# Query loads moved from ScalarE's queue to SyncE's and spread over the strip, the norm's arithmetic moved from GpSimd to VectorE, and the sums of W_in in another order

## The chip, the cores and the metric

The kernel runs on one core of a Trainium2 chip. A core has TensorE (PE, matrix products, with its weight loads shown apart as PEld), VectorE (DVE), ScalarE (ACT), GpSimd (POOL) and SyncE (SP, which here only issues DMAs). Each has its own instruction stream, and they meet at semaphores. An engine works through its stream in order, so an instruction that waits holds up all that stand behind it on the same engine. SBUF is the working memory, PSUM the memory into which PE writes its products; "HBM" is the memory outside.

The metric is device time in microseconds, the median of several runs. The profile is of one further run.

## The reference

Two blocks are chained. The first is linear attention without a softmax; each head's output is divided by its root mean square:

```python
kv = np.einsum('bhsd,bhse->bhde', k, v)
out = np.einsum('bhsd,bhde->bhse', q, kv)
rms = np.sqrt(np.mean(out * out, axis=-1, keepdims=True) + 1e-06)
return (out / rms * g_norm).astype(np.float32)
```

with 8 batches, 8 heads, 576 positions and 64 features. The heads of a position are put side by side, which gives x with 4608 rows and 512 columns. The second block is a feed-forward layer with 2048 hidden features:

```python
h = x @ w_in
r = np.maximum(h, 0.0)
g = r * r
return (g @ w_out).astype(np.float32)
```

All is in 32-bit floats; the two weight matrices come as 64-bit floats and are converted in the kernel.

## The kernel before

**Tiles and strips.** The 4608 rows of x are 36 tiles of 128 rows, and four tiles make a strip, so there are nine strips, numbered 0 to 8. For each strip the kernel computes h = x W_in (the first products, "up"), the squared relu, and g W_out (the second products, "down"). Both products use Strassen's scheme: seven products of half-size blocks in place of eight, at the price of sums of blocks. From strip 1 on the down products, and from strip 2 on the up products too, use it twice over (`up_small`, `small_products`). Sums of weights are made once: `sums_in` (line 269) and `deep_sums_in` (line 1040) make those of W_in. The first are made by VectorE at the end of strip 0, after ScalarE has scaled W_in by the norm's weight. The second are made by GpSimd in strip 1 and are written to HBM (`w_in_deep`). Weight blocks (`w_blk`) stream back in through four buffers, by SyncE.

**Attention inside the strips.** While PE works through strip s, the attention for strip s+1 is done in between. It is cut into small slices, a list `slices` of functions with arguments; after each step of a strip, `attend` (line 680) runs as many slices as are due. In strips from 2 on a step of the up products is called a slot (`up_slot`), and all slices are due within the first 37 of 55 slots. So all attention work falls into the up products. The slices for batch b are:

- `key_value`: k'v for two heads at a time, on PE; ScalarE copies it to SBUF (`kv_all`, lines 382 and 383). It then issues the load of the k and v that come two pairs later.
- `transposed_query(b, p)` (line 346): from batch 2 on VectorE transposes the queries of head pair p (line 350) from tile `q` to `qT`. Tile `q` has two buffers, so the load for a pair can't start until the pair two before it is transposed. The last quarter of a row tile has its queries in `q_rest`.
- `query(pair)`: the products of queries with k'v for two tiles (line 411, `x_ps`, one PSUM buffer), and their squares on ScalarE (line 420, `sq`).
- `mean_roots`: VectorE reduces the squares (line 428), GpSimd makes mean and epsilon (line 429), ScalarE takes the root (line 434, `rms`).
- `roots`: VectorE takes the reciprocal (line 440) and GpSimd does one Newton step in four small instructions (lines 441 to 444)[...].
- `normalized`: VectorE multiplies `x_ps` by the result (line 491), which frees `x_ps`.
- `squares_x`, `send_x`, `fetch_x`: a transposition in blocks on VectorE (line 558), a write to HBM and a read back (lines 567 and 573), which together put x into `xT` with features on the partitions.

**Query loads.** One pair's queries are four DMAs (`load`, line 121) and the `q_rest` of one batch eight (line 167). `load_queries` and `load_q_rest` are slices as well: `transposes` puts one of them into `later_q` for every transpose, and `turn` lets one out at a time among the other slices. They are issued on ScalarE's queue (`nc.scalar`). All DMAs of the program, whatever queue they are in, share eight semaphores in turn; a DMA is not issued until the one that had its semaphore before has landed.

**PSUM in the up products.** There are five banks for products (`fpsum`), one bank with tag "at", in which k'v products are made, and the two of `x_ps`. Each product's bank is emptied by ScalarE (line 1151, `snap`) or by VectorE (line 1146), and PE waits for that before it writes the bank again. GpSimd adds earlier results to some of the copies (line 1146) and makes the sums of x (`x_l`, `x_t`, line 262).

Lines 1206 and following are the loop over a strip's steps, with the calls of `attend`, `sums_in`, `sums_x` and `deep_sums_in`.

Of the kernel before, what the change touches and what calls it, by code (L numbers as in the profile page):

```python
# [10 lines left out]
FP32 = mybir.dt.float32  # L11
# [4 lines left out]
ALU = mybir.AluOpType  # L16
# [4 lines left out]
def kernel(  # L21
# [34 lines left out]
    nc = tc.nc  # L56
    P = 128
# [4 lines left out]
    NP = H // 2  # L62
# [37 lines left out]

    main = {}

    def load(b, p, q_eng, names="kvq"):
        hs = slice(2 * p, 2 * p + 2)
        inputs = (("q", q, q_eng), ("k", k, nc.sync), ("v", v, nc.sync))
        if b == 0 and p >= 2:

            h_place = g_pool.tile([P, 4, C * P], FP32, name="first_qkv", tag="gt")
        if b == 1 and p == 2:
            h_place = spare_pool.tile([P, 3, C * P], FP32, name="more_qkv")  # L110
        placed = (b, p) in ((0, 2), (0, 3), (1, 2))
        for i, (n, src, eng) in enumerate(inputs if b == 0 else inputs[1:] + inputs[:1]):
            if n not in names:
                continue
            whole = src[b, hs, 0 : C * P].rearrange("h (sp c) d -> sp h c d", c=C)
            if n == "q" and b >= Q_ON_PE:

                t = qkv_pool.tile([P, 4 * C, SQ], FP32, name=n, tag=n)
                for a in range(4):
                    h, f = divmod(a * SQ, D)  # L120
                    eng.dma_start(
                        out=t[ts(a, SQ)],
                        in_=src[b, 2 * p + h, 0 : C * P, f : f + SQ].rearrange("(i k) f -> i k f", k=4 * C),
                    )
            elif n != "q":
                if placed:
                    t = h_place[:, i].rearrange("p (h c d) -> p h c d", h=2, c=C)
                else:
                    t = qkv_pool.tile([P, 2, C, D], FP32, name=n, tag=n)
                eng.dma_start(out=t, in_=whole)  # L130
            else:

                if placed:
                    t = h_place[:, i].rearrange("p (c h d) -> p c h d", h=2, c=C)
                else:
                    t = qkv_pool.tile([P, C, 2, D], FP32, name=n, tag=n)
# [15 lines left out]
        for t, src in ((k_rest[half], k), (v_rest[half, h], v)):  # L152
            eng.dma_start(out=t, in_=src[b, :, C * P : S].rearrange("h s d -> s h d"))

    def load_q_rest(b, eng, half=None):
        h = b % 2
        if h == 0 and not half:
            q_rest[b // 2] = rest_pool.tile([P, H, D], FP32, name="q_rest", tag="q_rest")
        src = q[b, :, C * P : S]
        if b < Q_ON_PE:  # L160
            eng.dma_start(out=q_rest[b // 2][REST * h : REST * (h + 1)], in_=src.rearrange("h s d -> s h d"))
            return
        t = squares(q_rest[b // 2])
        for a in range(*((0, 4) if half is None else (2 * half, 2 * half + 2))):
            hq, f = divmod(a * SQ, D)
            for kq in range(2):
                eng.dma_start(
                    out=t[ts(a, SQ), 2 * h + kq], in_=src[hq::2, ts(kq, SQ), f : f + SQ].rearrange("p i f -> i p f")
                )
# [9 lines left out]
            load(*u, q_eng, names)  # L179
            owed.extend([u] if "q" not in names else [])  # L180

    def load_queries():
        if owed:
            load(*owed.popleft(), nc.scalar, "q")


    KH, FH, DH = NP // 2, d_ff // 2, d_model // 2
# [156 lines left out]
            nc.tensor.matmul(ps, lhsT=ident, rhs=ident[:, : ps.shape[1]], start=True, stop=True)  # L344

    def transposed_query(b, p):
        t = main.pop(("q", b, p))
        if b >= Q_ON_PE:
            qT[b, p] = qt_pool.tile([P, C, P], FP32, name="qT", tag="qT")
            nc.vector.transpose(out=flat(qT[b, p]), in_=flat(t))  # L350
            if b % 2 and p == NP - 1:
                nc.vector.transpose(
                    out=open_rest(b).rearrange("p q (k t) -> p q k t", k=4),
                    in_=squares(q_rest[b // 2]).rearrange("p k q f -> p q k f"),
                )
            return
        ps = apsum.tile([P, C, P], FP32, name="t_ps", tag="at")
        if (b, p) == (0, 0):
            keep_busy(ps[:, 0], 8)
        for c in range(C):  # L360
            nc.tensor.transpose(ps[:, c, :], flat(t[:, c]), ident)
        qT[b, p] = qt_pool.tile([P, C, P], FP32, name="qT", tag="qT")
        nc.scalar.copy(qT[b, p], ps)
# [56 lines left out]
            nc.scalar.activation(sqs[-1], ps, AF.Square)  # L420
        return sqs

    def mean_of(sqs, eng=nc.vector):
        ms = small.tile([P, 2, H], FP32, name="ms", tag="ms")[:, : len(sqs)]
        for i, sq in enumerate(sqs):
            if len(sq.shape) == 3:
                sq = sq.rearrange("p r e -> p (r e)")
            nc.vector.reduce_sum(out=ms[:, i], in_=by_head(sq), axis=AX.X)
        eng.tensor_scalar(out=ms, in0=ms, scalar1=1.0 / D, scalar2=EPS, op0=ALU.mult, op1=ALU.add)
        return ms  # L430

    def root_of(ms):
        r = small.tile([P, 2, H], FP32, name="rms", tag="rms")[:, : ms.shape[1]]
        nc.scalar.activation(r, ms, AF.Sqrt)
        return r

    def newton(ms, r):

        t = small.tile([P, 2, H], FP32, name="newton", tag="newton")[:, : ms.shape[1]]
        nc.vector.reciprocal(r, r)  # L440
        nc.gpsimd.tensor_tensor(out=t, in0=ms, in1=r, op=ALU.mult)
        nc.gpsimd.tensor_tensor(out=t, in0=t, in1=r, op=ALU.mult)
        nc.gpsimd.tensor_scalar(out=t, in0=t, scalar1=-0.5, scalar2=1.5, op0=ALU.mult, op1=ALU.add)
        nc.gpsimd.tensor_tensor(out=r, in0=t, in1=r, op=ALU.mult)
        return r

    def inverse_root(ms, r):
# [2 lines left out]

        nc.vector.scalar_tensor_tensor(out=t, in0=ms, scalar=-0.5, in1=r, op0=ALU.mult, op1=ALU.mult)
        nc.vector.tensor_tensor(out=t, in0=t, in1=r, op=ALU.mult)
        nc.vector.scalar_tensor_tensor(out=r, in0=t, scalar=1.5, in1=r, op0=ALU.add, op1=ALU.mult)
        return r

    queried = []

# [11 lines left out]

    def roots_normalized(ns):  # L470
        parts, ms = queried.pop()
        queried.append((parts, inverse_root(ms, root_of(ms))))
        normalized(ns)

    def mean_roots(ns):
        parts, sqs = queried.pop()
        ms = mean_of(sqs, nc.gpsimd)
        queried.append((parts, (ms, root_of(ms))))

    def roots(ns):  # L480
        parts, means = queried.pop()
        queried.append((parts, newton(*means)))

    def normalized(ns):
        parts, r = queried.pop()
        for i, n in enumerate(ns):
            x_n[n] = xn_pool.tile([P, d_model], FP32, name="x_n", tag="x_n")
            o = x_n[n].rearrange("p (q r d) -> p r q d", r=2, d=D)
# [134 lines left out]
    for pair in query_pairs(1):  # L623
        slices += [(query_means, (pair,)), (roots_normalized, (pair,))]
        for n in pair:
# [4 lines left out]
            slices.append((features, (n,)))  # L630
            if n % NT == NT - 1:
                ready[n // NT] = len(slices)
    load_q = (load_queries, ())
    later_q = deque()

    def transposes(b, ps_of):
        for p in ps_of:
            slices.append((transposed_query, (b, p)))
            later_q.append(load_q)
            if p == NP - 1 and b + 1 < B:  # L640
                later_q.extend((load_q_rest, (b + 1, nc.scalar, half)) for half in range(2))

    def turn(n=1):
        for _ in range(min(n, len(later_q))):
            slices.append(later_q.popleft())

    for b in range(2, B):
        if b > 3:
            fetch(2)
            transposes(b, (2, 3))  # L650
        else:
            for p in range(NP):
                turn()
                slices.append((key_value, (b, p)))
                transposes(b, (p,))
                fetch(1)
                if b == 2 and p == 0:
                    slices += late
        for i, pair in enumerate(query_pairs(b)):
            slices.append((query, (pair, *((b + 1, 2 * i, 2 * i + 1) if i < 2 < b < B - 1 else ()))))  # L660
            if i == (2 if b % 2 else 1) and 2 < b < B - 1:
                transposes(b + 1, (0, 1))
            else:
                turn()
            slices.append((mean_roots, (pair,)))
            fetch(1)
            turn()
            slices.append((roots, (pair,)))
            fetch(1)
            turn()  # L670
            slices.append((normalized, (pair,)))
            for n in pair:
                turn()
                slices.append((squares_x, (n,)))
            slices += [(send_x, (n,)) for n in pair]
            fetches.extend(pair)
    fetch(2)
# [506 lines left out]
    for s in range(N_STRIP):  # L1184
# [21 lines left out]
        for i, (w, fn, a) in enumerate(steps):  # L1206
# [26 lines left out]
                convert((3, 4, 5, 7)[i])  # L1233
            done += w
            if s:
                if s >= DEEP_UP:
                    attend(begun + (goal - begun) * min(i + 1, 37) // 37)
                else:
# [1 line left out]
                if s == DEEP and i == n_up - 3:  # L1240
                    leaf_sums(s, 4)
                if s == 1 and i in range(6, 27, 3):
                    deep_sums_in(i // 3 - 2)
                if s == 1 and i == n_up - 2:
                    stream(2)
                continue
# [4 lines left out]
            if i == n_up + 9:  # L1251
                load_rest(2, nc.sync)
                load_q_rest(2, nc.sync)
            if i - n_up in (7, 9, 10, 12):
                sums_in((i - n_up - 6) // 2)
            if i == n_up + 11:
                sums_x(1)
            n = i + 1 - (n_up - 6)
            pairs, m = divmod(max(n - 2 * NP, 0), 3)
# [34 lines left out]
```

## Time and profile before

| | us |
|---|---|
| median of 3 runs | 982.31 (980.74 to 984.03) |
| profiled run, span | 973.3 |
| PE busy | 903.6 |
| DVE busy | 722.6 |
| ACT busy | 319.4 |
| POOL busy | 322.2 |

How to read the profile: the span is divided among busy and idle time of each engine. An instruction that only waits, or that issues a DMA, does not count as busy; in the answers such work is marked with a q after the engine, as in ACTq. A group's or an instruction's arrow "<-" names what it waited for. "PEclk" is the clock that TensorE was granted, in tenths of full speed. "L1151" is line 1151 of the kernel. The page cuts the span into 40 slices of about 24.3 us. A strip from 2 on takes some 90 to 110 us, and of this the down products are about 39.

### The profile page before, as it was taken

How to read it: one execution, taken by the hardware profiler on the slowest of the kernel's cores; microseconds unless marked ns; L12 is line 12 of the kernel's file. 1: busy time of each engine (PE TensorE's matmuls, PEld its weight loads, DVE VectorE, ACT ScalarE, POOL GpSimd, SP SyncE). 2: the span in 40 equal slices, each digit the busy share in tenths (PEclk: the TensorE clock that was granted, in tenths of full speed). 3: DMA queues.
4: the chain of work that ended last, by engine and by line, in shares of the span. 5: the costliest groups of instructions: out<-in, count | busy, mean ns of one | idle time of the engine just before them, and what ended most of it. 6: DMA issues, size and time to landing. Idle time of an engine off the chain costs nothing.

```text
span 973.3 us, 20802 instructions
## 1 busy us (share of the span) xinstructions
PE 903.6 (93%) x8246; PEld 841.0 (86%) x8246; DVE 722.6 (74%) x1198; ACT 319.4 (33%) x646; POOL 322.2 (33%) x390
## 2 busy tenths in 40 slices
PE   6999996899978899889997999899899999999998
PEld 5434885789968898889997999799899999999998
DVE  3898978459836795558864896489568976895796
ACT  3796341230023701154023601270028014501720
POOL 0000003080417604352336404550456048315710
PEclk8999998999989999999998999899999999999999
DMA  9599997959897487776887687849755866685475
GB/s 279 210 290 297 308 345 225 218 203 331 305 247 195 166 311 251 189 210 232 300 211 213 218 321 229 215 157 331 222 176 178 315 223 218 231 315 195 141 278 188
DMA packets 173807, 235.72 MB, mean 242 GB/s; under 512 B 85008, under 2 KB 138768, under 8 KB 165264
## 3 DMA queue, kind: packets, MB, share of 16 engines
q1 hardware_dynamic: 121168, 227.84, 70.3%
q10 hardware_dynamic: 52544, 6.56, 4.7%
q8 instruction: 65, 1.06, 0.4%
q14 instruction: 30, 0.25, 0.1%
HBM read 197.66 MB, written 36.70 MB: 241 GB/s over the span
## 4 chain that ended last, share of the span: by engine, by line
PE 60%; DMA 13%; DVE 12%; POOL 4%; issue 4%; ACT 3%; SPq 2%; ACTq 2%; DVEq 0%; POOLq 0%
PE ps_B L946 19%; PE ps_A L946 15%; PE ps_A L1134 11%; PE ps_B L1134 5%; DMA q<-in_q_dram 4%; PE ps_C L1134 3%; DMA w_blk<-w_in_deep 2%; PE ps_A L725 2%; POOL gt L1146 2%; DVE w_t L262 2%; PE kv_ps L379 1%; DVE o_sb L961 1%; DVE w_c L242 1%; DMA v_rest<-in_v_dram 1%; DMA w_out<-w_in 1%
## 5 line engine op out<-in xcount | busy, mean ns | idle before, releaser
L1134 PE MATMUL ps_A<-x_l,w_in 128*128 128x128 f32 x784 | 109.3, 284 | 18.8 <-ACT snap L1151 18.5
L946 PE MATMUL ps_B<-w_blk,g_s 128*128 128x128 f32 x1024 | 126.0, 275 | 0.0
L946 PEld LDWEIGHTS ps_B<-w_blk,g_s 128*128 128x128 f32 x1024 | 120.0, 192 | 0.1
L1134 PEld LDWEIGHTS ps_A<-x_l,w_in 128*128 128x128 f32 x784 | 98.6, 197 | 21.7 <-ACT snap L1151 14.3
L946 PE MATMUL ps_B<-w_blk,gt 128*128 128x128 f32 x768 | 97.4, 275 | 0.0
L946 PE MATMUL ps_A<-w_blk,g_s 128*128 128x128 f32 x768 | 93.6, 275 | 0.0
L946 PEld LDWEIGHTS ps_B<-w_blk,gt 128*128 128x128 f32 x768 | 91.5, 192 | 0.1
L262 POOL TENSOR_TENSOR x_l<-xT 128x256 f32<-128x256 f32 x21 | 15.7, 748 | 223.4 <-PE ps_A L946 223.3
L946 PEld LDWEIGHTS ps_A<-w_blk,g_s 128*128 128x128 f32 x768 | 89.6, 192 | 0.0
L1151 ACT COPY snap<-ps_A 128x512 f32<-128x512 f32 x63 | 36.5, 582 | 153.9 <-PE ps_A L1134 89.4
L1146 POOL TENSOR_TENSOR snap<-snap,gt 128x512 f32<-128x512 f32 x35 | 45.9, 1312 | 118.5 <-ACT snap L1151 79.8
L961 DVE TENSOR_TENSOR o_sb<-o_sb,ps_B 128x256 f32<-128x256 f32 (+1 forms) x128 | 49.5, 387 | 35.4 <-ACT o_sb L962 27.9
L1084 ACT ACTIVATE gt<-gt 128x512 f32<-128x512 f32 x112 | 69.6, 622 | 15.3 <-DVE gt L1146 11.0
L946 PE MATMUL ps_A<-w_blk,gt 128*128 128x128 f32 x576 | 72.2, 275 | 0.0
L1085 ACT ACTIVATE gt<-gt 128x512 f32<-128x512 f32 x112 | 70.6, 631 | 3.6
L946 PEld LDWEIGHTS ps_A<-w_blk,gt 128*128 128x128 f32 x576 | 68.2, 192 | 0.0
L1044 POOL TENSOR_TENSOR w_i<-w_in 128x512 f32<-128x512 f32 x7 | 9.8, 1394 | 156.2 <-PE kv_ps L379 153.8
L262 DVE TENSOR_TENSOR gt<-gt 128x2048 f32<-128x2048 f32 (+1 forms) x29 | 59.7, 2063 | 0.0
L1146 POOL TENSOR_TENSOR gt<-gt,snap 128x512 f32<-128x512 f32 x42 | 52.4, 1276 | 16.0 <-DVE snap L1146 15.8
L1134 PE MATMUL ps_A<-x_l,w_blk 128*128 128x128 f32 x392 | 53.8, 281 | 3.8 <-POOL x_l L262 3.8
L962 ACT COPY o_sb<-ps_A 128x128 f32<-128x128 f32 x24 | 6.4, 266 | 146.0 <-PE ps_A L946 146.0
L1134 PEld LDWEIGHTS ps_A<-x_l,w_blk 128*128 128x128 f32 x392 | 49.2, 197 | 4.8 <-POOL x_l L262 4.3
(177 smaller groups left out, 1856.3 us busy)
## 6 DMA issues: line engine op xcount, KB each, us to landing
w_blk<-w_deep SPq DMA_DIRECT2D x56, 1024.0 KB, 6.4
w_blk<-w_out SPq DMA_DIRECT2D x56, 768.0 KB, 5.7
w_blk<-w_in_deep SPq DMA_DIRECT2D x49, 768.0 KB, 5.2
raw<-in_moe_w_in_dram SPq DMA_DIRECT2D x16, 512.0 KB, 6.5
raw<-in_moe_w_out_dram SPq DMA_DIRECT2D x16, 512.0 KB, 5.9
k<-in_k_dram SPq DMA_DIRECT2D x29, 256.0 KB, 4.8
v<-in_v_dram SPq DMA_DIRECT2D x29, 256.0 KB, 5.0
x_d<-x_q SPq DMA_DIRECT2D x27, 256.0 KB, 3.3
```

What stands on the lines that cost most here:

```text
L242: yield nc.vector.scalar_tensor_tensor(out=ci, in0=high, scalar=-(2**30), in1=ci, op0=ALU.bitwise_and, op1=ALU.bitwise_or)
L262: eng.tensor_tensor(out=out, in0=a, in1=b, op=ALU.subtract)
L379: nc.tensor.matmul(ps[ts(h, D), i], lhsT=a, rhs=w, start=c == 0, stop=c == C)
L725: nc.tensor.matmul(bank[BANK[p]][:, i, :], lhsT=lhsT(k), rhs=rhs(k), start=p in (1, 5, 2) and i == 0 and k == 0, stop=k == n - 1, skip_gro ...
L946: nc.tensor.matmul(chain[c][x][:, i, :], lhsT=a[:, f, :], rhs=w[:, f, :], start=x not in opened[c] and f == 0, stop=f == FQ // 2 - 1, skip ...
L961: add = lambda out, a, b: nc.vector.tensor_tensor(out=out, in0=a, in1=b, op=ALU.add)
L1044: nc.gpsimd.tensor_tensor(out=s1, in0=w_half(b, 0, 1), in1=w_half(b, 1, 1), op=ALU.add)
L1084: nc.scalar.activation(o, o, AF.Relu)
L1085: nc.scalar.activation(o, o, AF.Square)
L1134: nc.tensor.matmul(ps[:, i, :], lhsT=w, rhs=rhs, start=j in (1, 2, 5) and i == 0, stop=True, skip_group_check=True)
L1146: add = lambda eng, out, a, b: eng.tensor_tensor(out=out, in0=a, in1=b, op=ALU.add)
L1151: nc.scalar.copy(t, ps)
```

## The change

There are three parts.

1. Query loads go to SyncE's queue. They are no longer slices. Each transpose of a pair puts the load of the next pair that is owed into a queue `drips`, in two halves of two DMAs each; the last transpose of a batch puts in the next batch's `q_rest`, in four parts of two DMAs. At every second step of a strip, up and down products alike, `drip` lets one part out. A transpose lets out what it needs itself if that is still waiting. The aim is to keep DMA issues off ScalarE and to spread them.
2. The mean, epsilon and the Newton step are done on VectorE. The slice `roots` is gone, and its work is done in `normalized`. ScalarE writes the root into PSUM, in the bank with tag "at". The aim is a shorter chain between engines.
3. Sums of W_in. `sums_in` of the four groups comes after down steps 7, 8, 9 and 11 of strip 0, where it was 7, 9, 10 and 12, and the sums of x come after step 12, where it was 11. `deep_sums_in` takes the seven blocks in the order 1, 6, 5, 4, 0, 2, 3.

```diff
-    def load_queries():
+    drips = deque()
+
+    def drip(n=1):
+        for _ in range(min(n, len(drips))):
+            f, a = drips.popleft()
+            f(*a)
+
+    def drip_queries():
         if owed:
-            load(*owed.popleft(), nc.scalar, "q")
+            u = owed.popleft()
+            drips.extend((load, (*u, nc.sync, "q", (2 * h, 2 * h + 1))) for h in range(2))
...
     def transposed_query(b, p):
+        while any(a[:2] == (b, p) for _, a in drips):
+            drip()
         t = main.pop(("q", b, p))
...
             if b % 2 and p == NP - 1:
+                while any(f is load_q_rest and a[0] == b for f, a in drips):
+                    drip()
...
+            drip_queries()
+            if p == NP - 1 and b + 1 < B:
+                drips.extend((load_q_rest, (b + 1, nc.sync, a)) for a in range(4))
             return
...
-    def mean_of(sqs, eng=nc.vector):
+    def mean_of(sqs):
...
-        eng.tensor_scalar(out=ms, in0=ms, scalar1=1.0 / D, scalar2=EPS, op0=ALU.mult, op1=ALU.add)
+        nc.vector.tensor_scalar(out=ms, in0=ms, scalar1=1.0 / D, scalar2=EPS, op0=ALU.mult, op1=ALU.add)
...
-    def newton(ms, r):
-
-        t = small.tile([P, 2, H], FP32, name="newton", tag="newton")[:, : ms.shape[1]]
-        nc.vector.reciprocal(r, r)
-        nc.gpsimd.tensor_tensor(out=t, in0=ms, in1=r, op=ALU.mult)
-        nc.gpsimd.tensor_tensor(out=t, in0=t, in1=r, op=ALU.mult)
-        nc.gpsimd.tensor_scalar(out=t, in0=t, scalar1=-0.5, scalar2=1.5, op0=ALU.mult, op1=ALU.add)
-        nc.gpsimd.tensor_tensor(out=r, in0=t, in1=r, op=ALU.mult)
-        return r
...
     def mean_roots(ns):
         parts, sqs = queried.pop()
-        ms = mean_of(sqs, nc.gpsimd)
-        queried.append((parts, (ms, root_of(ms))))
-
-    def roots(ns):
+        ms = mean_of(sqs)
+        r = apsum.tile([P, 2, H], FP32, name="root", tag="at")[:, : len(ns)]
+        queried.append((parts, (ms, root_of(ms, r))))
+
+    def normalized(ns):
         parts, means = queried.pop()
-        queried.append((parts, newton(*means)))
-
-    def normalized(ns):
-        parts, r = queried.pop()
+        r = inverse_root(*means)
...
             if s:
+                if i % 2 == (i >= n_up):
+                    drip()
...
                 if s == 1 and i in range(6, 27, 3):
-                    deep_sums_in(i // 3 - 2)
+                    deep_sums_in((1, 6, 5, 4, 0, 2, 3)[i // 3 - 2])
...
-            if i - n_up in (7, 9, 10, 12):
-                sums_in((i - n_up - 6) // 2)
-            if i == n_up + 11:
+            if i - n_up in (7, 8, 9, 11):
+                sums_in((7, 8, 9, 11).index(i - n_up))
+            if i == n_up + 12:
                 sums_x(1)
```

More of the change, by code (lines that the diff above doesn't have):

```diff
@@ L101, with load @@
     main = {}
-    def load(b, p, q_eng, names="kvq"):
+    def load(b, p, q_eng, names="kvq", parts=range(4)):
         hs = slice(2 * p, 2 * p + 2)
@@ L116, in load @@
             if n == "q" and b >= Q_ON_PE:
-                t = qkv_pool.tile([P, 4 * C, SQ], FP32, name=n, tag=n)
-                for a in range(4):
+                t = qkv_pool.tile([P, 4 * C, SQ], FP32, name=n, tag=n) if 0 in parts else main[n, b, p]
+                for a in parts:
                     h, f = divmod(a * SQ, D)
@@ L153, in load_rest, with load_q_rest @@
             eng.dma_start(out=t, in_=src[b, :, C * P : S].rearrange("h s d -> s h d"))
-    def load_q_rest(b, eng, half=None):
+    def load_q_rest(b, eng, one=None):
         h = b % 2
-        if h == 0 and not half:
+        if h == 0 and not one:
             q_rest[b // 2] = rest_pool.tile([P, H, D], FP32, name="q_rest", tag="q_rest")
@@ L163, in load_q_rest @@
         t = squares(q_rest[b // 2])
-        for a in range(*((0, 4) if half is None else (2 * half, 2 * half + 2))):
+        for a in range(4) if one is None else (one,):
             hq, f = divmod(a * SQ, D)
@@ L428, in mean_of, with root_of @@
             nc.vector.reduce_sum(out=ms[:, i], in_=by_head(sq), axis=AX.X)
-        eng.tensor_scalar(out=ms, in0=ms, scalar1=1.0 / D, scalar2=EPS, op0=ALU.mult, op1=ALU.add)
+        nc.vector.tensor_scalar(out=ms, in0=ms, scalar1=1.0 / D, scalar2=EPS, op0=ALU.mult, op1=ALU.add)
         return ms
-    def root_of(ms):
-        r = small.tile([P, 2, H], FP32, name="rms", tag="rms")[:, : ms.shape[1]]
+    def root_of(ms, ps=None):
+        r = ps if ps is not None else small.tile([P, 2, H], FP32, name="rms", tag="rms")[:, : ms.shape[1]]
         nc.scalar.activation(r, ms, AF.Sqrt)
-        return r
-    def newton(ms, r):
-        t = small.tile([P, 2, H], FP32, name="newton", tag="newton")[:, : ms.shape[1]]
-        nc.vector.reciprocal(r, r)
-        nc.gpsimd.tensor_tensor(out=t, in0=ms, in1=r, op=ALU.mult)
-        nc.gpsimd.tensor_tensor(out=t, in0=t, in1=r, op=ALU.mult)
-        nc.gpsimd.tensor_scalar(out=t, in0=t, scalar1=-0.5, scalar2=1.5, op0=ALU.mult, op1=ALU.add)
-        nc.gpsimd.tensor_tensor(out=r, in0=t, in1=r, op=ALU.mult)
         return r
@@ L452, in inverse_root @@
         nc.vector.tensor_tensor(out=t, in0=t, in1=r, op=ALU.mult)
-        nc.vector.scalar_tensor_tensor(out=r, in0=t, scalar=1.5, in1=r, op0=ALU.add, op1=ALU.mult)
-        return r
+        nc.vector.scalar_tensor_tensor(out=t, in0=t, scalar=1.5, in1=r, op0=ALU.add, op1=ALU.mult)
+        return t
     queried = []
@@ L471, in roots_normalized @@
         parts, ms = queried.pop()
-        queried.append((parts, inverse_root(ms, root_of(ms))))
+        queried.append((parts, (ms, root_of(ms))))
         normalized(ns)
@@ L632 @@
                 ready[n // NT] = len(slices)
[L633 to L645, printed above, removed]
     for b in range(2, B):
@@ L649 @@
             fetch(2)
-            transposes(b, (2, 3))
+            slices += [(transposed_query, (b, p)) for p in (2, 3)]
         else:
             for p in range(NP):
-                turn()
-                slices.append((key_value, (b, p)))
-                transposes(b, (p,))
+                slices += [(key_value, (b, p)), (transposed_query, (b, p))]
                 fetch(1)
@@ L661 @@
             if i == (2 if b % 2 else 1) and 2 < b < B - 1:
-                transposes(b + 1, (0, 1))
-            else:
-                turn()
+                slices += [(transposed_query, (b + 1, p)) for p in (0, 1)]
             slices.append((mean_roots, (pair,)))
             fetch(1)
-            turn()
-            slices.append((roots, (pair,)))
+            slices.append((normalized, (pair,)))
             fetch(1)
[L670 to L674, printed above, removed]
+            slices += [(squares_x, (n,)) for n in pair]
             slices += [(send_x, (n,)) for n in pair]
```

## The prediction

> **What bounds the kernel now.** I read the page first, then busy time by stage, then who waited for whom, then a stretch of instructions in order of time.
>
> ```profile
> PE 903.6 (93%) x8246; PEld 841.0 (86%) x8246; DVE 722.6 (74%) x1198; ACT 319.4 (33%) x646; POOL 322.2 (33%) x390
> ...
> PEclk8999998999989999999998999899999999999999
> ```
>
> TensorE (PE) is the bound at 93%, so time can only come from its idle 70 us and from slices in which its clock was not full. The stages say where these are (columns: length, then busy time of PE, weight loads, DVE, ACT, POOL, then the granted clock):
>
> ```profile
> 165.00:222.00 57.00, 51.38 (x407) 42.97 (x408) 29.48 (x44) 13.70 (x31) 25.48 (x27) 0.94 0.74 215
> 263.00:338.00 75.00, 62.86 (x740) 60.42 (x739) 43.03 (x70) 28.88 (x60) 42.27 (x52) 0.93 0.75 201
> 377.00:447.00 70.00, 59.44 (x643) 58.05 (x643) 39.55 (x65) 27.31 (x52) 33.43 (x47) 0.93 0.68 188
> 483.00:550.00 67.00, 60.91 (x671) 59.62 (x670) 43.35 (x69) 26.56 (x51) 35.62 (x46) 0.95 0.75 207
> 589.00:653.00 64.00, 59.04 (x681) 57.26 (x681) 43.92 (x71) 27.58 (x53) 33.07 (x44) 0.95 0.66 190
> 691.00:752.00 61.00, 55.01 (x575) 53.65 (x574) 41.24 (x66) 25.94 (x47) 33.05 (x44) 0.97 0.56 171
> 879.00:928.00 49.00, 49.00 (x441) 49.00 (x440) 32.45 (x48) 23.45 (x42) 31.04 (x33) 1.00 0.45 153
> ```
>
> These are the first products of strips 1 to 6 and, last, of strip 8. Strip 8 has no attention beside it and PE never stops. Strips 1 to 6 have attention beside them, and PE is idle 5.6, 12.1, 10.6, 6.1, 5.0 and 6.0 us. The second products (between these windows) are full. ACT's busy 29 of 75 us hides the cause, because issuing a DMA is not counted as busy. The waits show it:
>
> ```profile
> ACT rms L434 <- POOL ms L429: 33.6, 13, 4.3
> ACT snap L1151 <- DMA q<-in_q_dram: 26.4, 6, 6.5
> ACT snap L1151 <- DMA q_rest<-in_q_dram: 20.0, 4, 7.1
> ...
> PE ps_A L1134 <- ACT snap L1151: 18.5, 10, 4.2
> ```
>
> and one case in order of time, first ACT, then PE:
>
> ```profile
> 402.57 3.64 ACTq L121 DMA_DIRECT2D q<-in_q_dram  x4
> 406.25 0.59 ACT L1151 COPY snap<-ps_A 128x512 f32<-128x512 f32 x1 [4.66 <-issue]
> ...
> 402.21 1.06 PE L1134 MATMUL ps_A<-x_t,w_in 128*128 128x128 f32 x8
> 406.89 1.49 PE L1134 MATMUL ps_A<-x_l,w_in 128*128 128x128 f32 x7 [3.62 <-ACT snap L1151]
> ```
>
> ACT spends 3.64 us on four query loads; the copy that empties bank A stands behind them; PE, which needs the bank, stops for 3.62 us.
>
> **What the skill says.** "DMA: Bandwidth & Descriptors", section Issuing engines are not separate DMA queues: issuing from several engines saves only sequencer time, usually small beside the transfer. Here it isn't small: 88 query issues of median 637 ns and 40 of 443 ns are 74 us of ACT. "TensorE: Matmul & The Clock Gate", What's actually happening: an idle window drops the array to half clock and it takes a busy window to return. The trace agrees: the eight matmuls after the 3.05 us gap at 322.83 take 2.05 us on the chain of waits, while a usual eight take 0.89. "SBUF — State Buffer", Who interferes with whom: a VectorE instruction with two SBUF inputs contends with GpSimd's reads, one with a single SBUF input does not. The trace agrees: L451 (two small SBUF inputs) has a median of 168 ns and took 999 at 163.7, while GpSimd summed W_in.
>
> **The change part by part.**
>
> *Query loads leave ACT.* Going through every PE gap above 0.4 us after 165 us (42.1 in sum) and its releaser, I put to query issues or a query that came late: strip 1 2.93; strip 2 0.42, 4.53, 2.64; strip 3 2.36, 3.62, 4.22; strip 4 0.49, 3.23, 2.16; strip 5 0.41, 3.21, 0.54, 0.62; strip 6 3.51. That is 34.9 us. The clock lost, (1 − clock) × length over the six stages, is 3.4 + 5.3 + 4.9 + 3.4 + 3.2 + 1.8 = 22 us; in proportion to the gaps 18 of it belong here. The most to win is 53 us. I do not take all of it: behind each such wait stands another at a little distance (the bank copy also waits for output stores and for GpSimd's mean; x_l for GpSimd). Bounds: nothing, if the next wait ends just as late, and 53. I take 60%, **−32 us**.
>
> *They go to SyncE.* In the stage of strip 2 SyncE issues some 50 DMAs of about 0.4 us, 20 of 75 us; 24 issues of about 0.57 us add 14. So there is room, but the queue is in order: behind a query load that waits for its buffer (a transpose on DVE) stand the W_in blocks, x_d, xT, k and v; and a query load stands behind a block that waits for PE. In strips 2 to 6 a load is let out 3 or more slots (0.9 us each) ahead of its transpose, mostly 7 to 25, and the blocks have four buffers; I cost it inside the 60%. In **strip 1** it is tight: the loads of batch 2, pair 3, are forced out at the step of the transpose itself, behind k, v, k_rest and v_rest, which wait for the last k'v product. Before, that product ended near 181.1 and v_rest was issued by 184.8, 3.7 us later. Four issues (the last starts 1.9 later) and a landing of 4.2 put the data at +9.8, the transpose (0.7) at +10.5; PE has two steps of 1.8 until it reaches the query product that needs it. So PE stands some 7 us, plus 1.5 for the clock: **+8.5 us**. Lower bound 0, if SyncE runs ahead, upper bound 12.
>
> *Norms.* 15 pairs. GpSimd loses five instructions each of 0.20 to 0.26 us (L429, L441 to L444), 17 us in sum, none of it on PE's path as such. ACT loses its wait for GpSimd's mean (33.6 us), gets one for DVE's mean, which comes right after the reduction. Of PE's gaps only 3.05 at 322.83 runs through it (the chain: GpSimd mean, root, relus, copy), 4 with its clock. DVE gains four instructions of 0.17 us, 0.68 a pair, 10.2 in sum, beside 40 of 61 to 75 us busy; PE waits for DVE little (its own gaps name it for 3.2, 2.4 and 1.4), so I take 1 us on the path. The trace of before has no root in PSUM; both reads are bounded by 0.17 and by 1.0 each, the contended row, and having one SBUF input I take 0.17. Sum **−3 us**. The root takes the bank that k'v products use, but the next query product waits for the normalisation anyhow, since its own bank is single.
>
> *Sums of W_in.* The same instructions in another order. At 159.77 PE stands 7.13 us for x_n, because DVE is behind (8.17 of the 9 us from 159 to 168 busy). Three W_in sums there took 4.99 against 2.02 before, with GpSimd's first sum beside them. The new first piece (index 1) is the one DVE writes last, so GpSimd starts after them; but then it meets the sums of w_t or x_t that now come later. Between −5 and +3; I take **0**.
>
> Sum: −32 + 8.5 − 3 + 0 = −26.5; 982.3 − 26.5 = **956**.
>
> **Rivals.** (1) *All of the wait goes*, and strip 1 is not late: −53 − 4 + 8 = 933 with the strip 1 stall, about 925 without; for it speaks that strips 7 and 8 run with no idle PE, against it that strip 6, with only 8 loads on ACT, still takes 61 us where strip 8 takes 49. (2) *SyncE takes the place of ACT*: output stores and W_in blocks come later behind query loads, and the bank copy waits for stores ("ACT snap <- DMA out_dram" is already 14.8 us). A third of the gain is left, 53/3 = 18, minus 8.5, plus 3: about 970. (3) *Slower*: the late load of strip 1 comes back in all six batches of queries, 6 × 8.5 = 51, against a gain of 35: 982 + 16 = 998. For it: the query, not the copy, is what PE would then wait for, and two loads at a time reach into the next slots. Against it: the distances from strip 2 on are longer, and DVE waited for a query only once before (2.4 us).
>
> **How the numbers follow.** Forecast 0.58, all of it 0.12, SyncE 0.15, slower 0.15. Range 936 to 984: it takes in SyncE's case, nearly all of the forecast's spread (0 to 12 in strip 1, 45 to 75% of the gain) and about half of the first rival, and leaves out most of the slower one. Faster by over 0.3% (below 979.4): 0.58 + 0.12 + 0.12 = 0.82; within 0.3%: 0.05; slower 0.13.
>
> **What would show it.** Right: no query issues on ACT; "ACT snap <- DMA q" and "q_rest" gone; the stages of strips 2 to 4 shorter by 5 to 10 us each, with a clock nearer 1; strip 1 not shorter, with a gap before the query product some 9 steps in, released by a transpose of q. Wrong: PE waiting for query transposes in strips 2 to 6, W_in blocks or stores landing late behind query loads, or the same PE gaps released by another wait of the bank copies.

## The result and the profile after

The changed kernel takes 943.55 us (median of 4 runs, 939.37 to 947.33), the kernel before 983.17 beside it (4 runs, 980.74 to 987.08). The ratio is 0.959, with a 95% interval of 0.954 to 0.965: 39.6 us less, where 26.5 had been forecast. A repetition on another chip gave 0.962 (0.959 to 0.966).

The page of the changed kernel, its first two parts, engine by engine and the granted clock:

```profile
span 943.6 us, 20804 instructions
PE 894.6 (95%) x8246; PEld 833.3 (88%) x8246; DVE 736.8 (78%) x1258; ACT 318.6 (34%) x646; POOL 305.8 (32%) x315
...
PEclk7999899899998999999999999899999999999999
```

VectorE is busy 14 us longer and still far from being the bound; GpSimd is busy 16 us less with 75 instructions fewer. PE runs the same 8246 matmuls in 9 us less, which fits its higher clock (below), and sits idle 49 us instead of 70.

The stages, with the same columns as in the prediction. The windows follow the same products, up to their rough edges, so they begin at other times and are as long as these products take:

```profile
165.00:222.00 57.00, 50.22 (x392) 41.49 (x393) 28.05 (x47) 13.46 (x30) 23.27 (x18) 0.91 0.72 210
266.00:334.00 68.00, 59.93 (x740) 57.98 (x739) 46.59 (x78) 28.42 (x59) 40.50 (x41) 0.95 0.85 228
371.00:430.00 59.00, 55.78 (x651) 54.35 (x651) 45.03 (x80) 26.81 (x52) 32.86 (x35) 1.00 0.84 229
476.00:535.00 59.00, 55.87 (x641) 54.74 (x640) 44.32 (x77) 28.28 (x53) 28.30 (x28) 0.97 0.73 214
580.00:643.00 63.00, 58.58 (x658) 57.65 (x658) 46.95 (x82) 27.78 (x54) 28.25 (x28) 0.95 0.76 213
686.00:738.00 52.00, 52.00 (x572) 51.53 (x571) 45.11 (x75) 25.88 (x48) 25.39 (x24) 1.00 0.62 214
```

The windows of strips 2 to 6 are shorter by 7, 11, 8, 1 and 9 us, that of strip 1 by nothing; strip 6 now runs without idle time. The edges matter for strip 4, whose window holds 641 matmuls where it held 671. Counted in both traces from the middle of one strip's down products to the middle of the next strip's, strips 2 to 6 are shorter by 6.9, 11.9, 4.8, 1.1 and 8.6 us, and the middle of strip 1's is reached 3.1 us later (246.8 instead of 243.7 us).

Length minus PE's busy time, summed over the first six, fell from 45.4 to 25.6 us; (1 − clock) × length fell from 22 to 13.5. Together that is 28 us, close to the 29.7 between the two spans (973.3 and 943.6). The profiled run of before was a short one: it took 975.4 us where the median is 983.2, while that of the changed kernel, at 945.4, is near its median of 943.55 (a span is some 2 us shorter than the time of its run). Experiment 4, which runs in the same time as the kernel before, has a span of 981.1, and its strip 3 suggests what the short run lacked:

```profile
381.00:455.00 74.00, 60.15 (x649) 58.83 (x647) 39.49 (x65) 27.32 (x52) 33.80 (x48) 0.91 0.66 178
```

Here PE is idle 13.9 us at a clock of 0.91, against 10.6 and 0.93 in the profile of before and 3.2 and 1.00 after.

The waits of the changed kernel:

```profile
ACT root L449 <- DVE ms L444: 25.3, 13, 5.0
ACT snap L1131 <- DMA out_dram<-o_sb: 11.7, 4, 2.9
PE x_ps L426 <- DVE qT_rest L364: 6.9, 2, 6.7
PE kv_ps L394 <- DMA v<-in_v_dram: 5.6, 4, 2.5
PE x_ps L426 <- DVE qT L360: 5.3, 1, 5.3
PE ps_A L1114 <- ACT snap L1131: 1.1, 2, 0.6
```

Of the waits "ACT snap <- DMA q" and "q_rest" (46.4 us) 2.6 us are left, and PE's wait for bank A fell from 18.5 to 1.1. The bank copy's wait for output stores did not grow (14.8 before, 11.7 after), so there is no sign that SyncE's queue holds the stores up more than it did. PE's waits for data grew: for a query from 3.2 to 5.3, for `q_rest` from 1.4 to 6.9 and for v from 0.6 to 5.6; that for weight blocks of the down products (`w_blk`) went from 0.4 to 2.8. The query in strip 1 in order of time, SyncE's issues, then VectorE, then PE:

```profile
180.41 0.63 SPq L153 DMA_DIRECT2D v_rest<-in_v_dram  x1
181.14 4.00 SPq L121 DMA_DIRECT2D q<-in_q_dram  x4
187.06 0.71 DVE L360 STREAM_TRANSPOSE qT<-q 128x512 f32<-128x512 f32 x1 [5.46 <-DMA q<-in_q_dram]
187.91 0.71 PE L426 MATMUL x_ps<-kv_all,qT 64*64 64x64 f32 x16 [5.26 <-DVE qT L360]
```

This is the stall that the prediction named: four query loads right behind v_rest (k, v and k_rest went out from 178.07 on), VectorE waiting for them, PE waiting for VectorE. Strip 2 repeats it:

```profile
283.95 0.71 DVE L360 STREAM_TRANSPOSE qT<-q 128x512 f32<-128x512 f32 x1 [5.49 <-DMA q<-in_q_dram]
285.31 0.49 PE L426 MATMUL x_ps<-kv_all,qT_rest 64*64 64x64 f32 x8 [6.69 <-DVE qT_rest L364]
```

The line that PE names is `qT_rest`, but what was late is the query before it: VectorE stood 5.49 us for that one and transposed `q_rest` right after it.

### The profile page after: what moved, and what is told of

It reads as the page before. It is cut to its first block, busy times and chain, and to the rows that moved or that the text cites. A ratio compares the mean times of both kernels' runs of the same rounds, so it can differ in the third digit from the quotient of the medians.

```text
span 943.6 us, 20804 instructions
## 1 busy us (share of the span) xinstructions
PE 894.6 (95%) x8246; PEld 833.3 (88%) x8246; DVE 736.8 (78%) x1258; ACT 318.6 (34%) x646; POOL 305.8 (32%) x315
## 4 chain that ended last, share of the span: by engine, by line
PE 74%; DVE 11%; DMA 8%; SPq 2%; issue 2%; ACT 2%; DVEq 0%; ACTq 0%
PE ps_B L926 21%; PE ps_A L1114 16%; PE ps_A L926 16%; PE ps_B L1114 8%; PE ps_C L1114 4%; PE ps_A L705 3%; DVE w_c L250 2%; PE kv_ps L394 1%; DMA v<-in_v_dram 1%; PE x_ps L426 1%; DMA q<-in_q_dram 1%; DMA w_blk<-w_deep 1%; PE ps_B L705 1%; DMA w_out<-w_in 1%; DVE w_t L270 1%
## 5 line engine op out<-in xcount | busy, mean ns | idle before, releaser
L1114 PE MATMUL ps_A<-x_l,w_in 128*128 128x128 f32 x784 | 106.1, 279 | 2.2 <-ACT snap L1131 1.1
L1126 DVE TENSOR_TENSOR gt<-ps_A,gt 128x512 f32<-128x512 f32 x49 | 32.9, 684 | 27.5 <-PE ps_A L1114 27.2
```

What stands on the lines that cost most here:

```text
L1114: nc.tensor.matmul(ps[:, i, :], lhsT=w, rhs=rhs, start=j in (1, 2, 5) and i == 0, stop=True, skip_group_check=True)
L1126: add = lambda eng, out, a, b: eng.tensor_tensor(out=out, in0=a, in1=b, op=ALU.add)
```

## The experiments

The theory at this point: the gain is that the loads left ScalarE's queue, and the norms add little. The rivals: the norms, or the order of the sums, or the mere spreading of the loads in time bring it. Ratios are to the kernel before on the same chip.

**1. The change again**, with no edit, beside experiments 10 to 12.

> The changed kernel itself once more, beside the next three on the same chip: 943 us (939 to 947), PE gaps of 5 to 7 us before the query products of strips 1 and 2.

Measured 943.44, 0.962 (0.959 to 0.966).

**2. The loads alone.** Part 1 of the change; norms and sums of W_in as before. Against the changed kernel:

```diff
-        ms = mean_of(sqs)
-        r = apsum.tile([P, 2, H], FP32, name="root", tag="at")[:, : len(ns)]
-        queried.append((parts, (ms, root_of(ms, r))))
+        ms = mean_of(sqs, nc.gpsimd)
+        queried.append((parts, (ms, root_of(ms))))
...
-                    deep_sums_in((1, 6, 5, 4, 0, 2, 3)[i // 3 - 2])
+                    deep_sums_in(i // 3 - 2)
```

(with `newton`, `roots`, and the steps of `sums_in` as before.)

> The kernel before with the loads of the change alone (SyncE, spread); norms and sums of W_in as before. My theory (the issues on ACT held PE up, the norms are worth 3 us): 948 us, nearly the whole gain, with the 5.3 us and 6.7 us gaps before the query products of strips 1 and 2 as in the changed kernel. Rival (norms on GpSimd hold ACT up: its wait for GpSimd's mean was 33.6 us): the loads alone give half or less, 963 us or more, and PE then waits for bank copies behind the root.

Measured 957.56, 0.972 (0.969 to 0.976): −27, between what the theory and the rival asked. The loads bring most, but not all. In its waits ScalarE still stands for GpSimd's mean, and the late queries are there:

```profile
ACT rms L449 <- POOL ms L444: 29.8, 13, 4.8
PE x_ps L426 <- DVE qT_rest L364: 8.5, 2, 7.4
PE x_ps L426 <- DVE qT L360: 7.1, 2, 5.4
```

**3. The norms alone.** Part 2 of the change; loads and order as before. Against the kernel before:

```diff
-        ms = mean_of(sqs, nc.gpsimd)
-        queried.append((parts, (ms, root_of(ms))))
+        ms = mean_of(sqs)
+        r = apsum.tile([P, 2, H], FP32, name="root", tag="at")[:, : len(ns)]
+        queried.append((parts, (ms, root_of(ms, r))))
...
-            slices.append((roots, (pair,)))
...
```

> The kernel before with the norms of the change alone; query loads stay on ACT. My theory: 980 us (3 us gained), the wait of ACT for the mean falls from 33.6 to about 25 us, and PE's gaps behind query issues stay at about 35 us. Rival (the chain between engines costs as much as the loads): 965 us or less.

Measured 973.69, 0.989 (0.983 to 0.994): −11, more than I had given the norms, less than the rival asked. ScalarE's wait for the query loads is untouched (29.9 us for `q` in this trace, 26.4 before), and so is PE's for the bank (18.5 before):

```profile
PE ps_A L1121 <- ACT snap L1138: 21.5, 7, 7.2
```

**4. The order alone.** Part 3 of the change, against the kernel before:

```diff
-                    deep_sums_in(i // 3 - 2)
+                    deep_sums_in((1, 6, 5, 4, 0, 2, 3)[i // 3 - 2])
...
-            if i - n_up in (7, 9, 10, 12):
-                sums_in((i - n_up - 6) // 2)
-            if i == n_up + 11:
+            if i - n_up in (7, 8, 9, 11):
+                sums_in((7, 8, 9, 11).index(i - n_up))
+            if i == n_up + 12:
                 sums_x(1)
```

> The kernel before with the new order of the sums of W_in alone. My theory: within 3 us of the kernel before, the gap of 7.1 us before the last transposition of x at 167 us becomes two gaps of about the same sum or some 3 us less. Rival (the order takes contention between VectorE and GpSimd away for good): 5 us or more faster.

Measured 984.85, 0.9989 (0.9966 to 1.0012): nothing. One gap of PE does get smaller, that for x_n: 7.1 us in the kernel before, 3.2 with the order alone. The time stays all the same. From 100 us to the first product of strip 2 PE's gaps sum to 11.6 us in the kernel before and 10.7 here: most of it comes back as other waits. The three parts alone sum to −27 − 11 − 1 = −39 us, which is the whole (39.6). Each has an interval of 2 to 5 us to either side, so an overlap of a few us isn't excluded.

**5. Same halves, same places, but issued by ScalarE.** Against the changed kernel:

```diff
-            drips.extend((load, (*u, nc.sync, "q", (2 * h, 2 * h + 1))) for h in range(2))
+            drips.extend((load, (*u, nc.scalar, "q", (2 * h, 2 * h + 1))) for h in range(2))
...
-                drips.extend((load_q_rest, (b + 1, nc.sync, a)) for a in range(4))
+                drips.extend((load_q_rest, (b + 1, nc.scalar, a)) for a in range(4))
```

> The changed kernel with the same query loads at the same places, let out in the same halves, but issued by ACT. It separates the queue from the spreading. My theory (the issue itself on ACT holds the bank copies up): 970 to 980 us, ACT waits for its own query issues again. Rival (what counts is that loads come in halves and spread, whatever the queue): 945 to 950 us.

Measured 961.87, 0.976 (0.972 to 0.980), between the two expectations. With the spreading kept, the queue is worth the distance to the change, 14 to 17 us by the ratios. What is left of the change here is −23 us, of which the norms are 11 (experiment 3); so spreading the loads in halves brings some 12, by subtraction, even on ScalarE's queue. PE's wait for the copy of bank A lies between the two kernels (18.5 before, 1.1 after):

```profile
PE ps_A L1114 <- ACT snap L1131: 10.2, 8, 3.4
```

**6. On SyncE, but all at once.** Every step lets out all that is waiting. Against the changed kernel:

```diff
-                if i % 2 == (i >= n_up):
-                    drip()
+                drip(len(drips))
```

> The changed kernel with all that waits in the queue of loads let out at the next step, on SyncE, so without spreading. My theory (leaving ACT's queue is most of the gain, and the spread costs in strips 1 and 2, where it makes two loads late): 938 to 946 us, the 5.3 and 6.7 us gaps before the query products of strips 1 and 2 shorter, some W_in blocks or stores later. Rival (the spread is what pays): 955 us or more, since the query loads stand in a lump ahead of blocks and stores on the same queue.

Measured 957.93, 0.977 (0.972 to 0.981): the rival is right, and without the spreading the change loses 14 to 17 us. The late queries do get better (PE's wait for `qT_rest` is 1.3, and strip 1's stall for `qT` is gone), but the lumps stand ahead of k and v on SyncE's queue. In strip 5 eight loads of `q` and eight of `q_rest` go out from 601.44 us on, and the k and v behind them only from 610.77:

```profile
PE kv_ps L394 <- DMA v<-in_v_dram: 28.0, 8, 11.5
```

The longest, 11.5 us, is that of strip 5. Queue and spreading are each worth about as much as the other, and each of them alone gets only about half of the 27 us (25 less the 11 of the norms here, 23 less 11 in experiment 5). Spreading means halves, later steps and the down products all at once; no run takes these apart, and none has the old slices on SyncE's queue.

**7. The root in SBUF.** The changed kernel with the norms on VectorE, but with ScalarE's root written to SBUF:

```diff
-        r = apsum.tile([P, 2, H], FP32, name="root", tag="at")[:, : len(ns)]
-        queried.append((parts, (ms, root_of(ms, r))))
+        queried.append((parts, (ms, root_of(ms))))
```

> The changed kernel with the root in SBUF instead of PSUM, nothing else. My theory (PSUM matters only while GpSimd reads SBUF; 15 pairs, two small instructions each that stretch from 0.17 to about 1 us when they meet it): up to 1 us per pair on VectorE, of which PE sees little, so 944 to 949 us. Rival (the place of the root is what made the norms cheaper than forecast): 952 us or more.

Measured 955.4, 0.973 (0.969 to 0.977): the rival is right. That is the time of experiment 2, in which the norms are not on VectorE at all: with the root in SBUF the move brings nothing that can be told, and where the root lies is worth 10 to 13 us. The first instruction of the Newton step in the table of groups (number, then minimum, median and maximum in ns), first with the root in SBUF (the 15 pairs and seven earlier ones), then in the changed kernel (the 15 pairs):

```profile
L456 DVE SCALAR_TENSOR_TENSOR newton<-ms,rms x22: 166/295/1237, 16.0 to 792.6; 128x16 f32<-128x16 f32 x14, 128x8 f32<-128x8 f32 x8
```

```profile
L456 DVE SCALAR_TENSOR_TENSOR newton<-ms,root x15: 161/171/172, 193.4 to 786.0; 128x16 f32<-128x16 f32 x12, 128x8 f32<-128x8 f32 x3
```

The same instruction on the same tiles takes up to 1237 ns with two inputs in SBUF and never over 172 with one in PSUM. The three instructions of the step, over the 15 pairs, sum to 22.9 us against 7.6. It agrees with the Trainium skill, "SBUF — State Buffer", section Who interferes with whom: a VectorE instruction with two SBUF inputs shares a read port with GpSimd's reads. The trace shows it instruction by instruction: each of the 29 that took over 230 ns runs beside an instruction of GpSimd and ends 22 to 34 ns after that one's end. In the changed kernel 29 of the 45 lie wholly within an instruction of GpSimd, and none is stretched. ScalarE's root is a little shorter as well (216 ns into SBUF, 187 into PSUM, medians).

How a delay on VectorE gets to PE can be followed in strip 3. With the root in SBUF, GpSimd, then VectorE, then PE:

```profile
398.23 1.27 POOL L1125 TENSOR_TENSOR snap<-snap,gt 128x512 f32<-128x512 f32 x1 [5.95 <-DVE gt L1125]
399.45 1.27 POOL L270 TENSOR_TENSOR x_t<-xT,x_t 128x512 f32<-128x512 f32 x1
398.29 1.24 DVE L456 SCALAR_TENSOR_TENSOR newton<-ms,rms 128x16 f32<-128x16 f32 x1
399.56 1.20 DVE L457 TENSOR_TENSOR newton<-newton,rms 128x16 f32<-128x16 f32 x1
400.79 0.65 DVE L458 SCALAR_TENSOR_TENSOR newton<-newton,rms 128x16 f32<-128x16 f32 x1
403.90 0.65 DVE L1125 TENSOR_TENSOR snap<-ps_B,gt 128x512 f32<-128x512 f32 x1
404.61 1.65 PE L1113 MATMUL ps_B<-x_t,w_blk 128*128 128x128 f32 x6 [2.74 <-DVE snap L1125]
```

and the same product in the changed kernel:

```profile
397.00 1.16 PE L1114 MATMUL ps_B<-x_t,w_blk 128*128 128x128 f32 x8 [0.18 <-DVE snap L1126]
```

GpSimd's first instruction here ends at 399.50, VectorE's first at 399.53. The step takes 3.09 us where it takes 0.51 in the changed kernel; VectorE works without a pause from there to the copy that empties bank B, and PE waits 2.56 us longer for that copy. Over the whole trace PE's waits for VectorE's copies of banks in the up products from strip 2 on (line 1125, or 1126) sum to 8.2 us against 2.6. The rest of the 10 to 13 us was not followed.

**8. Every step early on.** In strips 1 and 2 one part is let out at every step, to cure the late queries:

```diff
-                if i % 2 == (i >= n_up):
+                if s <= 2 or i % 2 == (i >= n_up):
```

> The changed kernel with a part of the loads let out at every step in strips 1 and 2, in place of every second, and as before from strip 3 on. My theory (two loads were late for their transposes there: PE stood 5.3 and 6.7 us): both gaps fall to 3 us or less, 935 us. Rival (SyncE's order behind k and v, not the step, makes them late): the gaps stay, 943 us.

Measured 945.25, 0.963 (0.958 to 0.968), no gain. In the profile, which is of the longest of the six runs (952.34), the queries came earlier (PE's gaps for them 3.9 us, and no long one for `qT_rest`), k and v later:

```profile
PE kv_ps L394 <- DMA v<-in_v_dram: 8.8, 5, 3.1
PE kv_ps L394 <- DMA v_rest<-in_v_dram: 4.7, 2, 3.7
```

On one queue in order, what is let out earlier is paid for by what stands behind it.

**9. The mean on VectorE, the Newton step on GpSimd**, in a slice of its own and with the root in SBUF. Against the changed kernel:

```diff
...
+        nc.gpsimd.tensor_tensor(out=t, in0=ms, in1=r, op=ALU.mult)
+        nc.gpsimd.tensor_tensor(out=t, in0=t, in1=r, op=ALU.mult)
+        nc.gpsimd.tensor_scalar(out=t, in0=t, scalar1=-0.5, scalar2=1.5, op0=ALU.mult, op1=ALU.add)
+        nc.gpsimd.tensor_tensor(out=r, in0=t, in1=r, op=ALU.mult)
...
-            slices.append((normalized, (pair,)))
+            slices.append((roots, (pair,)))
+            slices.append((normalized, (pair,)))
```

> The changed kernel with the Newton step back on GpSimd (and its own slice), while mean and epsilon stay on VectorE; the root is in SBUF. It splits the 11 us that the norms alone gave. If ACT's wait for GpSimd's mean was the cost: 945 us, nearly as the changed kernel. If the Newton step's way through GpSimd was: 953 us or more, as the loads alone (957.6).

Measured 952.14, 0.969 (0.964 to 0.974). Between experiment 2 (mean and Newton step on GpSimd, 957.56) and the change (both on VectorE, 943.55), so taking the mean off GpSimd is worth some 3 to 5 us, with intervals that overlap, and the rest hangs on the Newton step and the root's place. By experiment 7 the Newton step on VectorE, with the root in SBUF, brings nothing over this (955.4).

**10. Fetches of x later.** In strips 3 to 6 (batches 4 to 7) k and v stand in SyncE's queue behind reads of x that themselves wait for a write; in strip 5 of the changed kernel SyncE stood 4.5 us for one. This puts two such reads behind the two transposes:

```diff
         if b > 3:
-            fetch(2)
             slices += [(transposed_query, (b, p)) for p in (2, 3)]
+            fetch(2)
```

> The changed kernel with the read back of x for two tiles placed behind the two transposes of queries, not ahead of them. In the changed kernel SyncE stood 4.5 us in strip 5 for a write of x that had only just been issued, and k and v behind it came late for PE (gaps of 2.5 and 2.0 us). My theory (the order on SyncE is now a bound in places): the two gaps go, 938 us. Rival (SyncE then waits elsewhere, or x comes late): 943 us or more.

Measured 939.04, 0.958 (0.954 to 0.962), the shortest of all. It is shorter than the kernel before for certain; against the change on the same chip (943.44, 0.959 to 0.966) the intervals overlap, so whether it gains is open. PE's wait for v fell from 5.6 us to 4.9, and the two gaps in strip 5, 2.46 and 1.96 in the profile of the change, are 1.46 and 1.00: smaller, not gone.

**11. The change with the old order of sums**, the reverse of experiment 4 on the changed kernel.

```diff
-                    deep_sums_in((1, 6, 5, 4, 0, 2, 3)[i // 3 - 2])
+                    deep_sums_in(i // 3 - 2)
...
```

(with the steps of `sums_in` and `sums_x` as before.)

> The changed kernel with the old order of the sums of W_in. Alone the new order gave nothing (ratio 0.999). My theory (it gives nothing with the rest either): 943 us. Rival (with the norms on VectorE it keeps GpSimd off VectorE's SBUF reads in strip 0 and 1): 948 us or more.

Measured 946.21, 0.965 (0.961 to 0.969); the median is 2.8 us above that of the change, the intervals overlap. As in experiment 4, PE's gap for x_n is larger with the old order (5.3 against 2.3 us); an effect of a few us isn't settled.

**12. The mean's input in PSUM too.** The sums of squares are reduced into PSUM, and the mean reads them there:

```diff
-            nc.vector.reduce_sum(out=ms[:, i], in_=by_head(sq), axis=AX.X)
+            nc.vector.reduce_sum(out=(ms if sums is None else sums)[:, i], in_=by_head(sq), axis=AX.X)
...
+        both = apsum.tile([P, 2, 2, H], FP32, name="root", tag="at")
+        ms, r = mean_of(sqs, both[:, 0, : len(ns)]), both[:, 1, : len(ns)]
```

> The changed kernel with the sums of squares reduced into PSUM too, in the bank of the root, so that the small instruction for mean and epsilon no longer reads SBUF. In the changed kernel that instruction took 6.4 us in 15 where 15 undisturbed ones take 2.6. If contention with GpSimd on a small instruction of this chain costs time as the three of the Newton step do (root in SBUF: 15.3 us more on VectorE, about 11 in the time): 2 to 3 us faster, 940 us. If not: 943 us or slower, since the bank is taken earlier.

Measured 944.3, 0.963 (0.960 to 0.967): no gain. The instruction did what was wanted. With the sums in PSUM, then in the changed kernel:

```profile
L444 DVE TENSOR_SCALAR ms<-root x15: 166/174/176, 190.5 to 778.8; 128x16 f32<-128x16 f32 x12, 128x8 f32<-128x8 f32 x3
```

```profile
L444 DVE TENSOR_SCALAR ms<-ms x22: 171/174/1094, 13.2 to 781.1; 128x16 f32<-128x16 f32 x14, 128x8 f32<-128x8 f32 x8
```

The stretched cases (up to 1094 ns, each ending 29 to 34 ns after an instruction of GpSimd) are gone; in the 15 pairs they had cost 6.4 us in sum, against some 2.6 at 0.174. So under 4 us of VectorE's time were saved, and the end didn't move.

## Why the prediction was right, and where it was short

The direction and the mechanism of the main term were right; 943.55 lies in the range, 12.4 us under the forecast of 956. The gain was 13 us larger than forecast.

**Query loads leave ACT, and go to SyncE: right.** The sum of its two terms was −32 + 8.5 = −23.5; experiment 2 gives −27. The wait for the loads was the cause, and most of PE's gaps that I had put to it did go. That the sum came within 4 us is luck in part: of the 53 us I took 60%, and no line of the trace stood behind that share. What the prediction did not take apart is how much the queue and how much the spreading bring: about half each (experiments 5 and 6). It argued the change as if the queue were all, and on SyncE with lumps it would have been off by 14 to 17 us. Rival 2, SyncE in ACT's place with a time near 970, describes what experiment 6 showed, in a milder form (957.93), and by k and v rather than by stores.

**Strip 1: right in sum.** A stall of some 7 us, plus 1.5 for the clock, was forecast. The stall is 5.26 us, and the clock costs more than 1.5: it is 0.50 from 186.2 to 193.0 us, of which some 5.1 us lie behind the stall, so about 2.5 us are lost. Together that is 7.8 us against 8.5. The loads were four behind v_rest, as said, though their issues took 4.00 us together where 2.3 had been taken. The window of the stage is no longer than before because it holds fewer matmuls (392 for 407) and because other gaps left it: two waits for bank copies (2.93 and 0.79 us) and most of what lay in it of PE's wait for x_n (1.9 us before, 0.2 after).

**Strips 2 to 6, "I cost it inside the 60%": partly wrong.** From product to product strips 2 to 4 shortened by 6.9, 11.9 and 4.8 us, against "5 to 10". But the distances were not enough in strip 2, where a query came late by 5.49 us and PE lost 6.69; and in strip 5, which got only 1 us shorter, k and v stood behind queries and reads of x (PE 2.46 and 1.96). So of rival 3's six late batches two came. The two terms together came out 3.5 us too small in spite of these new waits, which the interval of experiment 2 (3 us to either side) hardly tells from nothing; if anything the 60% was low.

**Norms, −3: the term that was mis-sized.** Alone they are worth 11 us (experiment 3), on top of the loads 10 to 13 (experiment 2 to the change). I had counted the one gap of PE whose chain names GpSimd's mean. That left out what the mean's way through GpSimd costs elsewhere (experiment 9: 3 to 5 us, not settled). It also treated the root in PSUM as an unknown to be bounded, when it was the point: I took 0.17 us for each read of it, which is right (0.161 to 0.173), but did not ask what the same instructions would cost without it. Experiment 7 says: with the root in SBUF the norms' gain is gone. The row that told it was in the prediction, L451 at 999 ns for a usual 168. The prediction also read the skill's section too simply: that an instruction with a single SBUF input does not contend leaves out the exception for modes that use both ports, and L444, with a single input, was stretched to 1094 ns. Why the norms alone shorten strip 6 by 5 us (54 us with 1.0 idle, 59 with the order alone) and strip 3 by only 1 (73 for 74) is not settled.

**Order of the sums, 0: right**, to 1 us. The x_n gap that I had hoped from and feared for did shrink, and other gaps took its place.

The sum: −23.5 became −27, −3 became −10 to −13, 0 stayed 0. Of the 13 us between forecast and result some 7 to 10 are the norms, the rest the loads.

## What to carry to other kernels

DMA issues on an engine that empties PSUM banks are not counted as busy and can still set the time of TensorE: look for the waits "copy <- DMA", then move the loads to a queue that computes nothing and let them out in small pieces, since a queue in order makes whatever stands behind a lump late. When small arithmetic goes from GpSimd to VectorE while GpSimd still works, look at the maximum of the duration, not the median, and put one of the two inputs into PSUM if a bank is free; it decided whether the move brought anything. And price a move by what every engine along its chain waits, not only by the gap of PE that names it.

## What the runs showed of the hardware

- A VectorE instruction on 128x16 elements, some 170 ns long, took up to 1237 ns with both inputs in SBUF while GpSimd worked, and 161 to 172 with one of them in PSUM (experiment 7 and the changed kernel). The stretched ones ended 22 to 34 ns after the GpSimd instruction beside them. That a tile this small is stretched sevenfold, and that the remedy is worth 10 to 13 us of a span of 950, I had not expected.
- One with a single SBUF input and an SBUF output (L444, multiply and add with constants) was stretched too, up to 1094 ns, and not (176 at most) when its input was in PSUM. The same section of the skill counts this kind among those that can take the port shared with GpSimd, in the modes that use both ports; here the remedy gained no time (experiment 12).
- Gaps of a few us cost clock beside their own length: over the six stages PE's idle time fell by 19.8 us and the clock's loss by a further 8.5 (a clock that is low while PE stands is counted in both). Short gaps are enough: in the changed kernel a clock of 0.50 for 3.4 us, 1.7 us lost, began about 1 us after a gap of 1.85 us (which ended at 526.40) and 0.5 us after one of 2.29 us (at 165.21).
